# Transposing blocks 7 to 36 of q and k by transfers on SyncE's queue, in a fused sliding-window attention and MLP-mixer kernel

## Chip, cores and metric

One core of one Trainium2 chip runs the whole program. The metric is the device time of one execution in microseconds (us). Three runs of the kernel before took 337.27, 339.30 and 339.14 us; their median is 339.14 us.

## What is computed

Two stages, of which the first feeds the second. Inputs q, k and v have the shape (8, 8, 576, 64): batch, heads, positions, head size.

```python
scores = scale * np.matmul(q, k.transpose(0, 1, 3, 2))
...
bias = slopes[:, None, None] * (-np.abs(rel).astype(np.float32))[None, :, :]
mask = (rel >= 0) & (rel < window)          # window = 128
...
return np.matmul(attn, v).astype(np.float32)
...
xt = x.transpose(0, 2, 1)                   # x: heads side by side, (8, 576, 512)
h = np.maximum(xt @ w_tok1, 0.0) @ w_tok2
u = x + h.transpose(0, 2, 1)
h2 = np.maximum(u @ w_ch1, 0.0) @ w_ch2
return (u + h2).astype(np.float32)
```

Attention looks back over at most 127 positions, so a block of 128 queries needs the keys and values of its own block and of the one before.

## The kernel before

**Blocks.** A sequence of 576 positions is four blocks of 128 and a tail of 64. Two batches make a pair, and their two tails share one block (`TAIL`). So there are nine blocks in a pair and 36 in all. The list `todo` fixes their order (line 97: blocks 0, 1, 2, 3, 7, TAIL, 4, 5, 6 of a pair, then the next pair). This document numbers them 1 to 36 in that order. Blocks 1 to 9 are those of batches 0 and 1, blocks 10 to 18 those of batches 2 and 3, and so on. The key blocks that the attention of batch 0 needs are blocks 1 to 6, that of batch 1 adds 7 to 9.

**Loads.** `load` (lines 80 to 95) brings one block of q, k and v from HBM into `qld`, `kld` and a ring of 14 v tiles. All loads are issued by GpSimd (POOL), which also casts float32 to bfloat16 on the way. A q, k or v load of a full block writes 128 KB. The pool `ld` has 12 buffers for each of `qld` and `kld`, so a block's load waits until the transposes of the block twelve before have read their tile. At most eight of these transfers are under way, since each waits for the landing of the eighth before it.

**Transposes.** Scores need q and k with the head size on the partitions. `transposes` (lines 190 to 202) makes eight TensorE transposes of 128x128 into one PSUM tile `tp` (line 195) and one VectorE copy to the tile `qkT` in SBUF (line 201). The pool `tp` has eight buffers of `qkT`.

**Attention.** `scores` (line 204) multiplies keys by queries into PSUM (line 219), takes exp on ScalarE (line 228) and multiplies by a mask on VectorE (line 231). `values` multiplies by v (line 252) and normalises into the tile `xb` (lines 255, 257).

**Token mix and channel mix.** `token_mix(b)` runs over `xb` (matmuls `t1`, line 303, and `ht`, line 321), adds the residual on VectorE (`ub`, line 322) and transposes it (`ut`, line 327; copy `uT`, line 333). `channel_mix(b)` multiplies by WC1 into `ct` (line 347) or, for a tail, `cx` (line 356), applies Relu on ScalarE (line 349), multiplies by WC2 into `o2` (line 365), adds the residual on VectorE into the tile `ob` (line 369), and stores `ob` from SyncE's queue (SP; lines 372 and 374). The pool `op` has three `ob` tiles: the VectorE addition for a fourth block waits until the first block's store has landed. The PSUM pool `ps_m` has three buffers, shared by `t1`, `ht`, `ct`, `cx` and `o2`.

**Order of the work.** The program interleaves `channel_mix(b)` with attention and token mix of batch b+1 (`interleave`, line 386). A scheduler then sets the final order of every engine's instructions from times that it assumes for them; each engine runs its instructions strictly in that order. A transfer is issued by its engine as an instruction in the same order: SP and POOL stand still until the waits of the instruction at the head are met. In the kernel before, SP issues nothing but the 40 output stores.

Of the kernel before, what the change touches and what calls it, by code (L numbers as in the profile page):

```python
# [11 lines left out]
BF16 = mybir.dt.bfloat16  # L12
# [4 lines left out]
def kernel(  # L17
# [15 lines left out]
    nc = tc.nc  # L33
    P = nc.NUM_PARTITIONS
# [9 lines left out]
    NHP = H // 2  # L44
# [7 lines left out]
    HEADS = [[0, 2, 4, 6], [1, 3, 5, 7]]  # L52

    const = ctx.enter_context(tc.tile_pool(name="const", bufs=1))
    ld = ctx.enter_context(tc.tile_pool(name="ld", bufs=12))
    tpool = ctx.enter_context(tc.tile_pool(name="tp", bufs=8))
    ppool = ctx.enter_context(tc.tile_pool(name="pp", bufs=3))
    small = ctx.enter_context(tc.tile_pool(name="small", bufs=4))
    xpool = ctx.enter_context(tc.tile_pool(name="xp", bufs=2))
# [35 lines left out]
        return got  # L95

    ORDER = [0, 1, 2, 3, 7, TAIL, 4, 5, 6]
    todo = [(pr, blk) for pr in range(B // 2) for blk in ORDER]
    loaded = {}

    def load_to(n):
        while len(loaded) < min(n, len(todo)):
            key = todo[len(loaded)]
            loaded[key] = load(*key)
# [82 lines left out]
    qkT = {}  # L187
    xs = {}

    def transposes(pr, blk):  # L190
        got = loaded[pr, blk]
        tp = ps_o.tile([P, 2 * NHP, P], BF16, name="tp", tag="o")
        for i, t in enumerate(("q", "k")):
            for hp in range(NHP):
                nc.tensor.transpose(  # L195
                    tp[:, i * NHP + hp, :],
                    got[t][:, 2 * hp : 2 * hp + 2, :].rearrange("p h d -> p (h d)"),
                    ident[:, :],
                )
        t = tpool.tile([P, 2 * NHP, P], BF16, name="qkT", tag="qkT")  # L200
        nc.vector.tensor_copy(out=t[:, :, :], in_=tp[:, :, :])  # L201
        qkT[pr, blk] = t

    def scores(pr, blk):

        tail = blk == TAIL
        first = 0 if tail or blk % NC else 1
        me = qkT[pr, blk]
        sp = [ps_s[e].tile([P, 4, 2, P], F32, name=f"sp{e}", tag="s") for e in range(2)]

        work = [(1, blk, 0, P)]
        if tail:
            work += [(0, NC - 1, 0, R), (0, 2 * NC - 1, R, P)]
        elif not first:
            work += [(0, blk - 1, 0, P)]
        for i in range(4):
            for kind, kb, c0, c1 in work:
                for e in range(2):
                    nc.tensor.matmul(  # L219
                        sp[e][:, i, kind, c0:c1],  # L220
                        lhsT=qkT[pr, kb][e * D : (e + 1) * D, NHP + i, :],
                        rhs=me[e * D : (e + 1) * D, i, c0:c1],
                        start=True, stop=True,
                    )
        pb = []
        for e in range(2):
            pe = ppool.tile([P, 4, 2, P], BF16, name=f"pe{e}", tag=f"pe{e}")
            nc.scalar.activation(out=pe[:, :, first:, :], in_=sp[e][:, :, first:, :],  # L228
                                 func=ACT.Exp, scale=scale)
            mk = (maskt if tail else masks)[e]  # L230
            nc.vector.tensor_tensor(out=pe[:, :, first:, :], in0=pe[:, :, first:, :],  # L231
                                    in1=mk[:, :, first:, :], op=ALU.mult)
            pb.append(pe)
        return pb

    def values(pr, blk, e, pe):
        xb = xs[pr]
        tail = blk == TAIL
        vme = loaded[pr, blk]["v"]
        ot = ps_o.tile([P, 4, D + 1], F32, name="ot", tag="o")  # L240
        mms = [(slice(0, P), pe[:, i, 1, :], vme[:, h, :], i) for i, h in enumerate(HEADS[e])]
        if tail:
            for j in range(2):
                vb = loaded[pr, (j + 1) * NC - 1]["v"]
                for i, h in enumerate(HEADS[e]):
                    mms.append((slice(j * R, (j + 1) * R), pe[:, i, 0, j * R : (j + 1) * R],
                                vb[:, h, :], i))
        elif blk % NC:
            vb = loaded[pr, blk - 1]["v"]
            mms += [(slice(0, P), pe[:, i, 0, :], vb[:, h, :], i) for i, h in enumerate(HEADS[e])]  # L250
        for m, (to, l, r, i) in enumerate(mms):
            nc.tensor.matmul(ot[to, i, :], lhsT=l, rhs=r, start=m == 0, stop=m == len(mms) - 1,  # L252
                             skip_group_check=True)
        rt = small.tile([P, 4, 1], F32, name="rt", tag="rt")
        nc.vector.reciprocal(out=rt[:, :, :], in_=ot[:, :, D : D + 1])  # L255
        x4 = xb[:, blk, :].rearrange("p (i e d) -> p i e d", i=4, e=2)
        nc.vector.tensor_tensor(out=x4[:, :, e, :], in0=ot[:, :, 0:D],  # L257
                                in1=rt[:, :, :].broadcast_to([P, 4, D]), op=ALU.mult)
# [3 lines left out]
    def attention(b):  # L262
        pr, half = b // 2, b % 2
        if half == 0:
            xs[pr] = xpool.tile([P, NB, DM], BF16, name="xb", tag="xb")
        units = SCORE_ORDER[half]
        trs = [ORDER[:6], ORDER[6:]][half]
        n = pr * NB + (6 if half else 0)
        wait = list(trs)
        held = None  # L270
        for u in units + [None]:
            need = [] if u is None else ([u, 2 * NC - 1] if u == TAIL else [u])
            while any((pr, w) not in qkT for w in need):
                t = wait.pop(0)
                n += 1
                load_to(n + 7)
                transposes(pr, t)
                yield 450
            got = None
            if u is not None:  # L280
                got = (u, scores(pr, u))
                yield 700
            if held is not None:
                for e in range(2):
                    values(pr, held[0], e, held[1][e])
                    yield 300
            held = got
# [89 lines left out]
    def side(b):  # L377

        yield from attention(b)
        yield from token_mix(b)  # L380
# [21 lines left out]
    load_to(9)  # L402
    load_channel_weights(1)
    drain(attention(0))
    drain(token_mix(0))
    for b in range(B):
# [32 lines left out]
```

## Time and profile before

| | |
|---|---|
| median of three runs | 339.14 us (337.27 to 339.30) |
| the profiled execution's own time | 335.55 us |
| its span, first to last instruction | 333.8 us |
| granted TensorE clock, mean | 0.987 |
| busy: TensorE 303.6, VectorE 169.7, ScalarE 136.9, GpSimd 111.0 us | 91%, 51%, 41%, 33% of the span |
| moved by DMA | 27.81 MB in 121917 packets |

The profile is of one execution. PE is TensorE's matmuls, PEld its weight loads, DVE VectorE, ACT ScalarE, POOL GpSimd and SP SyncE; POOLq and SPq are those engines' instruction queues. In a row that groups instructions, the columns are: line, engine, operation, output<-input, shape and count; then busy time and the mean nanoseconds of one; then the idle time of the engine just before these instructions and what ended it. A row of the timeline has the start, the duration, and in brackets an idle gap before it. A matmul's duration in a row includes its pipeline, so the distance of two starts tells what one costs. In the strips of the page the span is cut into 40 slices of 8.35 us, and each digit is a share in tenths.

The program has three parts: up to 46.5 us the loads, the first attention and the first token mix; then channel mixes with the next batch's attention and token mix beside them, 33.4 and 40.8 us in turn; from 302.7 us the last channel mix alone.

### The profile page before, as it was taken

What the parts mean: (1) busy time and instruction counts of PE and PEld (TensorE: products, weight loads), DVE (VectorE), ACT (ScalarE), POOL (GpSimd) and SP (SyncE); (2) the same over time, 40 slices, a digit from 0 to 9 for tenths busy, and PEclk for the clock granted to TensorE, in tenths of its full rate; (3) what the DMA queues carried; (4) which work ended last, traced back from release to release, by engine and by line L of the source; (5) the groups of instructions that cost most, each with busy time, mean ns of one, the idle gap of its engine ahead of it and who ended that gap; (6) DMA issues with size and microseconds to landing.
All of it is one profiled execution on the core that took longest, in us unless ns stands there. A gap on an engine that the chain in (4) does not pass through costs nothing.

```text
span 333.8 us, 6457 instructions
## 1 busy us (share of the span) xinstructions
PE 303.6 (91%) x2688; PEld 162.6 (49%) x2688; DVE 169.7 (51%) x378; ACT 136.9 (41%) x213; POOL 111.0 (33%) x146
## 2 busy tenths in 40 slices
PE   2457769999999999999999999999999999999993
PEld 1234335545555555455565555455654555455541
DVE  2354456563665636474656546464656447461021
ACT  1653227702774038602863047504772057404600
POOL 8998565888786033303472000000000000000000
PEclk9999599999999999999999999999999999999998
DMA  9999999999999359914999220011000220011022
GB/s 74 136 114 167 170 195 161 139 117 189 174 105 131 75 110 77 67 44 101 73 85 83 81 78 3 0 63 66 2 2 13 83 63 2 0 65 63 2 76 82
DMA packets 121917, 27.81 MB, mean 83 GB/s; under 512 B 113824, under 2 KB 117280, under 8 KB 121888
## 3 DMA queue, kind: packets, MB, share of 16 engines
q0 software_dynamic: 116640, 17.97, 76.1%
q1 hardware_dynamic: 5248, 9.44, 8.2%
q8 instruction: 21, 0.34, 0.4%
q14 instruction: 8, 0.07, 0.1%
HBM read 35.91 MB, written 9.44 MB: 136 GB/s over the span
## 4 chain that ended last, share of the span: by engine, by line
PE 84%; DVE 7%; ACT 4%; issue 1%; DMA 1%; POOL 1%; POOLq 0%
PE o L365 28%; PE ct L347 23%; PE sp L219 7%; PE tp L195 6%; PE ot L252 6%; PE t L303 5%; PE ht L321 5%; PE cx L356 3%; PE ut L327 3%; ACT pe L228 2%; DVE xb L257 2%; DVE pe L231 2%; DVE ub L322 1%; DMA kld<-in_k_dram 1%; DVE qkT L201 1%
## 5 line engine op out<-in xcount | busy, mean ns | idle before, releaser
L349 ACT ACTIVATE r<-ct 128x512 bf16<-128x512 f32 x96 | 56.0, 601 | 133.9 <-PE ct L347 133.9
L347 PE MATMUL ct<-uT,WC 128*128 128x512 bf16 x384 | 98.0, 379 | 0.5 <-DVE uT L333 0.5
L365 PE MATMUL o<-WC,r 128*128 128x512 bf16 x384 | 95.4, 379 | 0.4
L228 ACT ACTIVATE pe<-sp 128x1024 bf16<-128x1024 f32 (+1 forms) x72 | 63.0, 926 | 27.3 <-PE sp L219 27.3
L365 PEld LDWEIGHTS <-r 128*128 128x128 bf16 x384 | 36.0, 98 | 37.6 <-issue 1.9
L91 POOL DMA_DIRECT2D qld<-in_q_dram x40 | 35.6, 891 | 45.3 <-PE tp L195 39.3
L369 DVE TENSOR_TENSOR ob<-o,ub 128x512 f32<-128x512 f32 x36 | 24.8, 690 | 48.1 <-PE o L365 48.1
L347 PEld LDWEIGHTS <-WC 128*128 128x128 bf16 x384 | 33.5, 98 | 28.0 <-issue 0.6
L231 DVE TENSOR_TENSOR pe<-pe,mask 128x1024 bf16<-128x1024 bf16 (+1 forms) x64 | 39.0, 619 | 12.1 <-ACT pe L228 8.0
L201 DVE COPY qkT<-tp 128x1024 bf16<-128x1024 bf16 x36 | 24.9, 692 | 31.5 <-PE tp L195 31.5
L94 POOL DMA_DIRECT2D v<-in_v_dram x40 | 35.0, 881 | 15.1 <-PE ot L252 6.2
L92 POOL DMA_DIRECT2D kld<-in_k_dram x40 | 35.4, 884 | 8.3 <-DMA WC<-in_moe_w_ch_dram 5.8
L322 DVE TENSOR_TENSOR ub<-ht,xb 128x512 bf16<-128x512 f32 x36 | 24.0, 688 | 27.1 <-PE ht L321 26.7
L252 PE MATMUL ot<-v,pe 128*128 128x65 bf16 (+1 forms) x544 | 30.4, 201 | 6.7 <-DVE pe L231 3.5
L252 PEld LDWEIGHTS <-pe 128*128 128x128 bf16 (+1 forms) x544 | 22.4, 102 | 26.6 <-DVE xb L257 17.1
L257 DVE TENSOR_TENSOR xb<-ot,rt 128x256 bf16<-128x256 f32 x72 | 30.6, 425 | 2.5
L219 PE MATMUL sp<-qkT 64*128 64x128 bf16 (+1 forms) x544 | 24.6, 224 | 4.0 <-DVE qkT L201 3.1
L255 DVE RECIPROCAL rt<-ot 128x4 f32<-128x4 f32 x72 | 12.9, 179 | 26.1 <-PE ot L252 25.5
L219 PEld LDWEIGHTS <-qkT 64*128 64x128 bf16 x544 | 17.6, 98 | 17.6 <-DVE qkT L201 16.6
L303 PE MATMUL t<-xb,W 128*128 128x512 bf16 x80 | 23.4, 402 | 0.8 <-DVE xb L257 0.8
L195 PE MATMUL tp<-ident,qld 128*128 128x128 bf16 x144 | 14.8, 228 | 9.1 <-DMA qld<-in_q_dram 5.0
L321 PE MATMUL ht<-r,W 128*128 128x512 bf16 x64 | 19.4, 398 | 0.3 <-ACT r L305 0.3
(46 smaller groups left out, 179.4 us busy)
## 6 DMA issues: line engine op xcount, KB each, us to landing
out_dram<-ob SPq DMA_DIRECT2D x32, 256.0 KB, 2.0
qld<-in_q_dram POOLq DMA_DIRECT2D x32, 128.0 KB, 5.5
kld<-in_k_dram POOLq DMA_DIRECT2D x32, 128.0 KB, 5.6
v<-in_v_dram POOLq DMA_DIRECT2D x32, 128.0 KB, 5.5
WC<-in_moe_w_ch_dram POOLq DMA_DIRECT2D x4, 768.0 KB, 10.4
out_dram<-ob SPq DMA_DIRECT2D x8, 128.0 KB, 2.3
qld<-in_q_dram POOLq DMA_DIRECT2D x8, 64.0 KB, 4.6
kld<-in_k_dram POOLq DMA_DIRECT2D x8, 64.0 KB, 4.2
```

The costliest lines, as they stand in the source:

```text
L91: nc.gpsimd.dma_start(out=got["q"][p0 : p0 + n, :, :], in_=rows(q, b, s0, n))
L92: nc.gpsimd.dma_start(out=got["k"][p0 : p0 + n, :, :], in_=rows(k, b, s0, n))
L219: nc.tensor.matmul(sp[e][:, i, kind, c0:c1], lhsT=qkT[pr, kb][e * D : (e + 1) * D, NHP + i, :], rhs=me[e * D : (e + 1) * D, i, c0:c1], sta ...
L228: nc.scalar.activation(out=pe[:, :, first:, :], in_=sp[e][:, :, first:, :], func=ACT.Exp, scale=scale)
L231: nc.vector.tensor_tensor(out=pe[:, :, first:, :], in0=pe[:, :, first:, :], in1=mk[:, :, first:, :], op=ALU.mult)
L252: nc.tensor.matmul(ot[to, i, :], lhsT=l, rhs=r, start=m == 0, stop=m == len(mms) - 1, skip_group_check=True)
L257: nc.vector.tensor_tensor(out=x4[:, :, e, :], in0=ot[:, :, 0:D], in1=rt[:, :, :].broadcast_to([P, 4, D]), op=ALU.mult)
L303: nc.tensor.matmul(t1[:, :], lhsT=W1[:, c, j * P : (j + 1) * P], rhs=xb[:, blk, :], start=n == 0, stop=n == len(ks) - 1)
L321: nc.tensor.matmul(ht[:, :], lhsT=l, rhs=r, start=n == 0, stop=n == len(mms) - 1)
L347: nc.tensor.matmul(ct[:, :], lhsT=WC1[:, cb, t * P : (t + 1) * P], rhs=uT[:, cb, :], start=cb == 0, stop=cb == NCB - 1)
L349: nc.scalar.activation(out=r2[:, t, :], in_=ct[:, :], func=ACT.Relu)
L365: nc.tensor.matmul(o2[:, :], lhsT=l, rhs=WC2[:, t, :], start=t == 0, stop=t == NHT - 1)
```

## The change

From block 7 on, TensorE's eight transposes and VectorE's copy of a block give way to two transposing transfers, one of q and one of k, each of a 128x512 bfloat16 tile in SBUF to half a `qkT` tile. SP issues them. They stand four blocks ahead of their use in the program's order. Blocks 1 to 6 stay as they were. `ld` has 9 buffers in place of 12, and `tp` 11 in place of 8.

```diff
-    ld = ctx.enter_context(tc.tile_pool(name="ld", bufs=12))
-    tpool = ctx.enter_context(tc.tile_pool(name="tp", bufs=8))
+    ld = ctx.enter_context(tc.tile_pool(name="ld", bufs=9))
+    tpool = ctx.enter_context(tc.tile_pool(name="tp", bufs=11))
...
+    EARLY = 6
...
+    moved = [EARLY]
+
+    def transpose_to(n):
+
+        while moved[0] < min(n, len(todo)):
+            key = todo[moved[0]]
+            moved[0] += 1
+            t = tpool.tile([P, 2 * NHP, P], BF16, name="qkT", tag="qkT")
+            for i, x in enumerate(("q", "k")):
+                nc.sync.dma_start_transpose(
+                    out=t[:, i * NHP : (i + 1) * NHP, :],
+                    in_=loaded[key][x][:, :, :].rearrange("p h d -> p (h d)"),
+                )
+            qkT[key] = t
...
-            while any((pr, w) not in qkT for w in need):
+            while any(w in wait for w in need):
                 t = wait.pop(0)
                 n += 1
                 load_to(n + 7)
-                transposes(pr, t)
-                yield 450
+                transpose_to(n + 4)
+                if (pr, t) not in qkT:
+                    transposes(pr, t)
+                    yield 450
```

The scheduler makes a new order of this. Three places of it matter below. Lines of the changed kernel are 1 to 18 higher than those of the kernel before: L214 is the transposing transfer, L235 the scores, L268 the values, L387 the addition into `ob`, L392 the store. In brackets stand the semaphores that an instruction waits for: DMAHW is the landing of a transfer that SP issued, DMASW of one that POOL issued, and the others are engines.

**SP, where the stores of batch 0 stand.** Before, SP's queue begins with them:

```order
L434 UNCONDITIONAL_BRANCH [waits barrier_Pool_Activation_PE_DVE_SP_release]
L374 DMA out_0_dram<-ob_961 128x512 [waits DVE_49]
L374 DMA out_0_dram<-ob_1011 128x512 [waits DVE_49]
L374 DMA out_0_dram<-ob_1033 128x512 [waits DVE_49]
L374 DMA out_0_dram<-ob_1049 128x512 [waits DVE_49]
```

Now 28 transposing transfers, of blocks 7 to 20, stand ahead of them; these are the last two of blocks 19 and 20 each, the four stores, and the first of block 21:

```order
L214 DMA_TRANSPOSE qkT_1294<-qld_1133 128x4x128 [waits DMAHW0_49,DMASW6_49,PE_49]
L214 DMA_TRANSPOSE qkT_1294<-kld_1134 128x4x128 [waits DMAHW1_49,DMASW7_49]
L214 DMA_TRANSPOSE qkT_1607<-qld_1213 128x4x128 [waits DMAHW2_49,DMASW0_49]
L214 DMA_TRANSPOSE qkT_1607<-kld_1214 128x4x128 [waits DMAHW3_49,DMASW1_49]
L392 DMA out_0_dram<-ob_965 128x512 [waits DMAHW4_49,DVE_49]
L392 DMA out_0_dram<-ob_1005 128x512 [waits DMAHW5_49,DVE_49]
L392 DMA out_0_dram<-ob_1021 128x512 [waits DMAHW6_49,DVE_49]
L392 DMA out_0_dram<-ob_1037 128x512 [waits DMAHW7_49,DVE_49]
L214 DMA_TRANSPOSE qkT_1640<-qld_1281 128x4x128 [waits DMAHW0_49,DMASW3_49,PE_49]
```

The store of `ob_965`, batch 0's first, comes behind the transfer of `kld_1214`, which waits (DMASW1) for the load of block 20's k.

**VectorE, at the end of batch 0's channel mix.** Before, the fourth addition into an `ob` tile is followed by the copies of blocks 10 and 11:

```order
L369 TENSOR_TENSOR ob_1033<-o2_1020,ub_562 128x512 [waits PE_49]
L369 TENSOR_TENSOR ob_1049<-o2_1036,ub_562 128x512 [waits DMAHW0_49,DVE_49,PE_49]
L201 COPY qkT_1075<-tp_1066 128x1024 [waits PE_49]
L201 COPY qkT_1113<-tp_1104 128x1024 [waits PE_49]
L231 TENSOR_TENSOR pe0_1087<-pe0_1087,mask0_141 128x4x128 [waits Activation_49]
```

Now:

```order
L387 TENSOR_TENSOR ob_1021<-o2_1008,ub_574 128x512 [waits PE_49]
L387 TENSOR_TENSOR ob_1037<-o2_1024,ub_574 128x512 [waits DMAHW4_49,DVE_49,PE_49]
L247 TENSOR_TENSOR pe0_1067<-pe0_1067,mask0_141 128x4x128 [waits Activation_49]
L247 TENSOR_TENSOR pe1_1070<-pe1_1070,mask1_142 128x4x128 [waits Activation_49]
L247 TENSOR_TENSOR pe0_1105<-pe0_1105,mask0_141 128x1024 [waits Activation_49]
```

The copies are gone. In both, the fourth addition waits for the landing of batch 0's first store (DMAHW0 before, DMAHW4 now).

**TensorE, at the values of block 4 in batch 0's attention.** Before, the second half of the heads follows the first at once:

```order
L252 MATMUL ot_506<-v2_98,pe0_412 128x65
L252 LDWEIGHTS pe0_412
L252 MATMUL ot_506<-v2_98,pe0_412 128x65
L252 LDWEIGHTS pe1_415 [waits DVE_49]
L252 MATMUL ot_518<-v3_99,pe1_415 128x65 [waits PE_49]
```

Now the scores of block 7 (`qkT_319`) stand between:

```order
L268 MATMUL ot_518<-v2_98,pe0_418 128x65
L235 LDWEIGHTS qkT_319 [waits DMAHW0_49,DMAHW1_49]
L235 MATMUL sp0_646<-qkT_319 128x128 [waits Activation_49]
L235 LDWEIGHTS qkT_319
L235 MATMUL sp0_646<-qkT_319 128x128
L268 LDWEIGHTS pe1_421 [waits DVE_49]
L268 MATMUL ot_530<-v3_99,pe1_421 128x65 [waits PE_49]
```

The scores of blocks 7, 8 and 9 all come ahead of batch 0's `ht` matmuls now; before, they came after the first `ct` matmuls.

## The prediction

> **What bounds the kernel now.** I read the page's busy times first, then the stages, then TensorE's timeline at a transposed block, and last the transfers.
>
> ```profile
> span 333.8 us, 6457 instructions
> PE 303.6 (91%) x2688; PEld 162.6 (49%) x2688; DVE 169.7 (51%) x378; ACT 136.9 (41%) x213; POOL 111.0 (33%) x146
> ```
> ```profile
> 34.00:41.00 7.00, 5.08 (x39) 2.24 (x36) 2.86 (x9) 1.75 (x3) 3.49 (x5) 0.55 2.10 170
> 46.50:80.10 33.60, 33.38 (x275) 17.14 (x275) 18.31 (x40) 14.46 (x22) 24.62 (x30) 1.00 2.07 153
> 80.10:120.90 40.80, 40.35 (x399) 22.23 (x398) 23.16 (x49) 17.98 (x27) 22.06 (x27) 1.00 1.52 128
> ```
>
> The second fence is the table by stage: stretch, its length, busy time of PE, PEld, DVE, ACT and POOL, the granted clock, the DMA share. From 46.5 us on, TensorE is busy for 99% of each stretch and VectorE for little more than half. So TensorE bounds the kernel there, and what leaves TensorE shortens it, if what replaces it is never late. Two blocks in TensorE's timeline:
>
> ```profile
> 33.78 0.42 PE L252 MATMUL ot<-v,pe 128*128 128x65 bf16 x8 [0.74 <-DVE xb L257]
> ...
> 39.46 2.91 PE L321 MATMUL ht<-r,W 128*128 128x512 bf16 x8 [0.26 <-ACT r L305]
> ...
> 46.51 1.02 PE L347 MATMUL ct<-uT,WC 128*128 128x512 bf16 x4 [0.52 <-DVE uT L333]
> ```
> ```profile
> 47.37 0.39 PE L195 MATMUL tp<-ident,qld 128*128 128x128 bf16 x4
> 47.59 0.39 PE L195 MATMUL tp<-ident,kld 128*128 128x128 bf16 x4
> 47.81 1.03 PE L347 MATMUL ct<-uT,WC 128*128 128x512 bf16 x4
> 48.77 0.40 PE L219 MATMUL sp<-qkT 64*128 64x128 bf16 x8
> 49.10 0.40 PE L195 MATMUL tp<-ident,qld 128*128 128x128 bf16 x4
> ```
>
> From the first of a block's eight transposes (47.37) to the next other matmul (47.81) is 0.44 us.
>
> **What the change removes.** Thirty blocks by 0.44 us is 13.2 us of TensorE. VectorE loses 30 copies:
>
> ```profile
> L201 DVE COPY qkT<-tp 128x1024 bf16<-128x1024 bf16 x36 | 24.9, 692 | 31.5 <-PE tp L195 31.5
> ```
>
> That is 20.8 us, which I count as nothing: VectorE is idle for almost half of each stage, and TensorE's matmuls already lie over it. Without that cover it would be worth up to those 20.8 us more.
>
> **What it adds: 60 transfers.** The trace has no transposing transfer, so I bound the cost on the DMA engines of one of 128 KB.
>
> ```profile
> q0 software_dynamic: 116640, 17.97, 76.1%
> q1 hardware_dynamic: 5248, 9.44, 8.2%
> ```
> ```profile
> GB/s 155 151 153 155 158 155 152 156 151 157 158 152 154 155 152 158 155 154 152 155 155 158 153 151 157 154 156 158 253 144 147 144 147 146 142 142 147 155 154 154
> ```
>
> The stores take 8.2% of 16 engines over 333.8 us, 27.4 us for 9.44 MB (36 times 256 KB): 0.76 us each, 0.38 us for 128 KB. The second fence is the transfer rate from 55 to 61 us, loads alone: 131,072 bytes at 155 GB/s is 0.85 us, in 1024 pieces of 128 bytes. If a transpose's time hides in gaps, its price is nothing. It moves 512 pieces of 256 bytes, half the load's pieces, hence 0.42 us, near the store's. I take 0.42, and keep 0 and 0.85 for the range. Advanced Engine Details and Errata (the Trainium skill, X-Bar Transpose) says that transposing transfers on this chip are as fast as plain ones, 350 to 400 GB/s; by it one would be 0.33 to 0.37 us, and the sum below about 2 us less; no run here shows it yet.
>
> **What it moves: SP's queue.** Before, SP only waited for results. Now batch 0's first store stands behind block 20's transposes, and those wait for block 20's loads. When do they land?
>
> ```profile
> 78.56 0.88 POOL L91 DMA_DIRECT2D qld<-in_q_dram  x1
> 79.69 0.89 POOL L92 DMA_DIRECT2D kld<-in_k_dram  x1 [0.24 <-issue]
> ```
> ```profile
> qld<-in_q_dram POOLq DMA_DIRECT2D x1, 128.0 KB, 8.4
> kld<-in_k_dram POOLq DMA_DIRECT2D x1, 128.0 KB, 8.3
> ```
> ```profile
> 70.67 48.71 SPq L374 DMA_DIRECT2D out_dram<-ob  x8
> 121.64 1.17 SPq L372 DMA_DIRECT2D out_dram<-ob  x2
> ```
>
> Block 20's k is issued at 79.69 and lands 8.3 us later, at 88.0; batch 0's first store was issued at 70.67. So the store waits for a load that lands 17 us after the store was wanted. POOL works with few gaps, so the loads cannot come much earlier. In the changed kernel: 88.0, less one v load that now follows (0.85), less the four stores that no longer precede (4 x 0.76 = 3.0), plus the 26 transposes of blocks 7 to 19 on the same engines (26 x 0.42 = 10.9): 95.0. Then the issue of the last transpose and of the store, 0.6 us (two issues in 1.17 us), and the store's flight:
>
> ```profile
> out_dram<-ob SPq DMA_DIRECT2D x4, 256.0 KB, 5.9
> ```
> ```profile
> out_dram<-ob SPq DMA_DIRECT2D x8, 256.0 KB, 2.0
> ```
>
> The first row is 70 to 81 us, with loads under way; the second 144 to 195 us, mostly without. Loads of blocks 21 to 25 are still going, so 5.9: the store lands at 101.5. Behind it stands VectorE: the fourth `ob` addition needs that landing (three buffers), and every mask and normalisation of the next attention is queued behind that addition. On TensorE the third `ct` group needs the PSUM buffer that the addition frees.
>
> ```profile
> 80.13 0.69 DVE L369 TENSOR_TENSOR ob<-o,ub 128x512 f32<-128x512 f32 x1 [1.90 <-PE o L365]
> ```
> ```profile
> 79.93 1.03 PE L347 MATMUL ct<-uT,WC 128*128 128x512 bf16 x4
> 80.79 0.39 PE L195 MATMUL tp<-ident,qld 128*128 128x128 bf16 x4
> ...
> 82.52 0.40 PE L195 MATMUL tp<-ident,qld 128*128 128x128 bf16 x4
> 82.76 0.39 PE L195 MATMUL tp<-ident,kld 128*128 128x128 bf16 x4
> 82.98 0.38 PE L347 MATMUL ct<-uT,WC 128*128 128x512 bf16 x1
> ```
>
> The third group began at 82.98. Now it begins at 101.5 + 0.7 = 102.2, 19.2 us late. After a stop TensorE runs slower: in 34 to 41 us above, with gaps, the granted clock was 0.55. I add 2 us for a restart (about 4 us at half speed, an estimate from that row; 0 to 3.5 in the range).
>
> **An earlier stop, inside the same delay.** TensorE reaches block 7's scores at about 33.8 us, before its loads have landed:
>
> ```profile
> 27.55 1.30 POOL L92 DMA_DIRECT2D kld<-in_k_dram  x1
> ...
> 37.49 0.87 POOL L92 DMA_DIRECT2D kld<-in_k_dram  x1 [2.86 <-DMA WC<-in_moe_w_ch_dram]
> ```
> ```profile
> kld<-in_k_dram POOLq DMA_DIRECT2D x2, 128.0 KB, 11.8
> ```
> ```profile
> kld<-in_k_dram POOLq DMA_DIRECT2D x1, 128.0 KB, 7.1
> ```
>
> Block 7's k lands at 27.55 + 11.8 = 39.4, block 9's at 37.49 + 7.1 = 44.6. With 4 us for a transpose's flight (between the store's 2.0 and 5.9), TensorE goes on at 43.4, 9.6 us late; block 9's transpose lands at 48.6, while the chain from 33.78 to 39.46 brings TensorE there at 49.1. Four masks of 0.69 us then stand in VectorE's chain to the first `ct`: 12.4 us late in all. Work that now lies before it is saved later: three blocks' transposes (1.3) and their scores with block 5's (0.33 for 8 matmuls, so about 2.0 for 56). With blocks 10 and 11 (0.9) the third `ct` group could start at 82.98 + 12.4 - 4.2 = 91.2. The store lands later than that, so this stop costs nothing of its own; without the blocked store it is what is left.
>
> **Later stores.** Batch 1's stand behind block 25's transposes, but were wanted only at
>
> ```profile
> 109.12 10.26 SPq L374 DMA_DIRECT2D out_dram<-ob  x4
> ```
>
> and come 20 us later now, while the first burst of loads ended by 117 us, the fourteenth slice of 8.35 us of the page's DMA strip:
>
> ```profile
> DMA  9999999999999359914999220011000220011022
> ```
>
> With the transposes it ends by about 128. From there on SP is ahead, and I cost later waits at nothing; each that came late would stop VectorE in the same way. The smaller `ld` pool makes POOL wait for SP's transposes, but of blocks some nine earlier, 24 us of loads at 0.88 us, so nothing; without that cover the loads would come later, as in the range's upper part.
>
> **The sum.** At the third `ct` group +19.2 + 2 = +21.2 us; from there 25 blocks (12 to 36) are saved, 25 x 0.44 = -11.0. Net +10.2. Against the profiled execution's own 335.55 us (1.75 outside its span) that is 345.8. The runs' median is 339.14, 3.6 above the profiled one, so I predict 339.14 + 10.2 = 349 us.
>
> **Rivals.**
> *No blocked store, only the early stop.* If transposes cost the DMA engines next to nothing and the store lands in 2 us, the third group starts at 91.2, plus 1 for the clock: +9.2 - 11.0 = -1.8, 337 us. For it: hidden loads leave gaps. Against it: with 0 for a transpose the store still waits for 84.2 (88.0 - 0.85 - 3.0), then 0.6 and 2 to 5.9.
> *The gain in full.* Both stops vanish and 13.2 us go: 326 us, faster. It needs block 20's k landed by 77 us, 7 to 18 sooner than the 84 to 95 above, and block 7's 8 to 10 sooner. Against it: POOL's issues, nearly back to back at 0.88 us. For it: TensorE's full stages.
> *The engines of the transfers become the bound.* If a transpose writes 32-byte strips, 4096 of them at the load's price a piece (0.85 / 1024), it takes 3.4 us. Block 20's k then lands at 84.1 + 26 x 3.4 = 172.5, the third group starts at 180: +97 + 2 - 11 = +88, 427 us. It decides above about 0.9 us each. Nothing in the trace speaks for strips; nothing excludes them. VectorE: DVE Perf Modes (the Trainium skill, The three transpose paths) gives 1309 ns for a 128x128 square by transfer against 390 ns on TensorE, and its rules for authors prefer TensorE where PSUM may be the target, as here. By that figure, if the four squares of a transfer ran one after the other, a transfer would be 5.2 us, an estimate beyond this rival's 3.4; no run here shows it yet.
>
> **How the numbers follow.** Blocked store: 0.68. Early stop only: 0.14. Full gain: 0.07. Transfers as the bound: 0.11. The blocked store's own range: at 0.2 us each and a 3 us store the third group starts at 93.6 (84.1 + 5.2 + 0.6 + 3 + 0.7), with 1 for the clock +0.6, 340; at 0.85 us it starts at 113.5, +21.5, 361. The early stop reaches down to 337, so 337 to 362 leaves out the full gain and dear transfers. About 1% (3.4 us) is what a measurement here can tell from no change. Faster by more: 0.07 and a fifth of the early stop, 0.10. Within it: the rest of the early stop and the low tenth of the blocked store, 0.18. Slower: 0.72.
>
> **What would show it.** Right: SP's first store of batch 0 issued 10 us or more after its `ob` is ready, VectorE waiting at L387 on a transfer for over 5 us near 90 to 102 us, TensorE idle there and at 34 to 43 us, and later pairs about 4 us shorter than 74.2 (33.4 + 40.8). Wrong: store 1 issued before 88 us; a transposing transfer that holds SP or the engines for over 1 us; later stages that do not shrink, which would mean that TensorE was not their bound.

## The result, and the profile after

The changed kernel takes 362.16 us (median of four runs, 360.00 to 363.28) against 338.31 us for the kernel before on the same chip: 1.0698 times as long, 95% interval 1.0633 to 1.0762. That is +23.9 us where +10.2 was forecast. The direction and the two stops are as forecast; most sizes are not. Its profiled execution took 362.28 us.

The page of the changed kernel, span, busy times and transfer queues:

```profile
span 360.5 us, 6047 instructions
PE 297.3 (82%) x2404; PEld 159.4 (44%) x2448; DVE 150.8 (42%) x348; ACT 137.7 (38%) x213; POOL 110.7 (31%) x146
...
q0 software_dynamic: 116640, 17.97, 76.9%
q1 hardware_dynamic: 37888, 17.31, 25.7%
```

TensorE has less work and a smaller share: 82% in place of 91%. The queue q1, which held stores alone, now carries 32,640 more packets, 544 for each of the 60 transfers.

The same execution by stage; each stretch runs from the first `ct` of one channel mix to that of the next (stretch, length, PE, PEld, DVE, ACT, POOL, granted clock, DMA share, GB/s):

```profile
0.00:71.01 71.01, 30.00 (x294) 18.80 (x299) 23.63 (x68) 21.18 (x35) 49.05 (x73) 1.00 1.76 139
71.01:99.84 28.83, 28.62 (x191) 13.78 (x195) 13.44 (x31) 9.87 (x16) 19.17 (x23) 1.00 2.04 150
99.84:153.79 53.95, 41.64 (x346) 23.12 (x350) 19.20 (x43) 18.34 (x27) 31.42 (x38) 0.84 2.11 162
153.79:186.27 32.48, 31.87 (x246) 16.28 (x250) 17.30 (x38) 14.51 (x22) 7.01 (x8) 1.00 1.05 119
186.27:225.21 38.94, 37.73 (x345) 20.87 (x350) 19.23 (x43) 17.91 (x27) 4.04 (x5) 1.00 0.54 82
```

The same table for two later stretches of the kernel before:

```profile
120.72:154.14 33.42, 33.20 (x275) 17.04 (x274) 19.00 (x41) 14.46 (x22) 8.77 (x10) 1.00 0.73 72
154.14:194.94 40.80, 40.35 (x400) 22.25 (x399) 23.16 (x49) 17.98 (x27) 15.47 (x19) 1.00 0.90 85
```

Before, the front took 46.51 us, and then came 33.42 and 40.79 us in turn. So the loss lies in two places: the front (+24.5 us) and the stretch from 99.84 us (+13.2). The stretch between them is 4.6 us shorter, since scores that stood in it now lie in the front and three blocks' transposes are gone. Each later stretch is shorter, by 0.95 us with three blocks in it and by 1.85 us with six: 0.31 us per block.

**First stop.** TensorE's timeline in the front:

```profile
39.93 0.62 PE L268 MATMUL ot<-v,pe 128*128 128x65 bf16 x8
50.12 0.39 PE L235 MATMUL sp<-qkT 64*128 64x128 bf16 x2 [9.57 <-DMA qkT<-kld]
...
57.12 0.71 PE L235 MATMUL sp<-qkT 64*128 64x128 bf16 x10 [3.57 <-DMA qkT<-kld]
...
61.83 1.03 PE L235 MATMUL sp<-qkT 64*128 64x128 bf16 x8 [1.50 <-DMA qkT<-kld]
...
71.01 2.32 PE L365 MATMUL ct<-uT,WC 128*128 128x512 bf16 x10 [0.55 <-DVE uT L351]
```

Three waits, each for the transpose of a `kld` tile: blocks 7, 8 and 9. The six transposes were issued at 39.7 to 47.8 us and landed 8.1, 9.1, 11.1, 12.2, 14.3 and 13.9 us later.

The granted clock of 1.00 that the table gives for the front does not fit TensorE's rows there:

```profile
37.16 0.59 PE L196 MATMUL tp<-ident,qld 128*128 128x128 bf16 x4
...
66.04 0.39 PE L345 MATMUL ut<-ident,ub 128*128 128x128 bf16 x4
```

Four transposes of 128x128 took 0.59 us at 37.16 and 0.39 from 66.04 on, and six `ht` matmuls from 62.79 us on started 0.42 us apart, where such matmuls later start 0.22 us apart. So TensorE seems to have run near half speed in much of the front, to about 65 us; what that cost is not measured.

**Second stop.** The chain of waits over the same execution, at block 20's transposes and batch 0's first store:

```profile
91.28 12.94 DMA qld<-in_q_dram
104.24 1.19 SPq L214
105.52 1.29 SPq L214
106.90 6.45 DMA out_dram<-ob
```

Block 20's load flies 12.9 us, SP issues the two transposes, 1.3 us apart, and only then the store. VectorE's timeline shows the first and the fourth addition:

```profile
91.29 0.69 DVE L387 TENSOR_TENSOR ob<-o,ub 128x512 f32<-128x512 f32 x1 [0.22 <-PE o L383]
...
113.47 0.69 DVE L387 TENSOR_TENSOR ob<-o,ub 128x512 f32<-128x512 f32 x1 [15.33 <-DMA out_dram<-ob]
```

and TensorE's timeline the third `ct` group behind it:

```profile
114.21 0.59 PE L365 MATMUL ct<-uT,WC 128*128 128x512 bf16 x1 [11.08 <-DVE ob L387]
```

The first `ob` was ready at 91.98; its store went out 14.9 us later. The table by stretch, TensorE alone, gives what followed the stop (the column before the DMA share is the granted clock):

```profile
106.10:114.20 8.10, 0.00 (x0) 0.50 1.72 202
114.20:123.20 9.00, 8.76 (x67) 0.50 2.02 175
123.20:130.00 6.80, 6.10 (x94) 1.00 2.22 149
```

After the stop TensorE ran 9.0 us at half clock, some 4.5 us lost (an estimate: half of 9.0).

### The profile page after: what moved, and what is told of

Its sections match the earlier page's. It is cut to its first block, busy times and chain, and to the rows that moved or that the text cites. A ratio compares the mean times of both kernels' runs of the same rounds, so it can differ in the third digit from the quotient of the medians.

```text
span 360.5 us, 6047 instructions
## 1 busy us (share of the span) xinstructions
PE 297.3 (82%) x2404; PEld 159.4 (44%) x2448; DVE 150.8 (42%) x348; ACT 137.7 (38%) x213; POOL 110.7 (31%) x146
## 4 chain that ended last, share of the span: by engine, by line
PE 54%; DMA 16%; POOL 9%; ACT 7%; issue 6%; DVE 5%; SPq 2%; ACTq 0%; POOLq 0%; DVEq 0%
PE o L383 23%; PE ct L365 13%; DMA qld<-in_q_dram 11%; ACT pe L244 6%; PE ht L339 4%; DMA qkT<-kld 4%; PE t L321 4%; PE ot L268 3%; DVE pe L247 3%; PE cx L374 3%; PE sp L235 3%; POOL v L94 2%; SPq L214 2%; POOL kld L92 2%; POOL qld L91 2%
## 5 line engine op out<-in xcount | busy, mean ns | idle before, releaser
L367 ACT ACTIVATE r<-ct 128x512 bf16<-128x512 f32 x96 | 57.0, 605 | 143.8 <-PE ct L365 139.0
L365 PE MATMUL ct<-uT,WC 128*128 128x512 bf16 x364 | 96.8, 384 | 13.1 <-DVE ob L387 11.1
L383 PE MATMUL o<-WC,r 128*128 128x512 bf16 x372 | 89.4, 379 | 0.6
L387 DVE TENSOR_TENSOR ob<-o,ub 128x512 f32<-128x512 f32 x36 | 24.9, 691 | 74.8 <-PE o L383 59.5
L235 PE MATMUL sp<-qkT 64*128 64x128 bf16 (+1 forms) x544 | 34.1, 235 | 18.4 <-DMA qkT<-kld 14.6
L235 PEld LDWEIGHTS <-qkT 64*128 64x128 bf16 x544 | 22.8, 104 | 35.7 <-DMA qkT<-kld 16.6
L268 PE MATMUL ot<-v,pe 128*128 128x65 bf16 (+1 forms) x544 | 31.4, 204 | 7.6 <-DVE xb L273 3.9
L268 PEld LDWEIGHTS <-pe 128*128 128x128 bf16 (+1 forms) x544 | 23.7, 105 | 24.1 <-DVE xb L273 14.5
L321 PE MATMUL t<-xb,W 128*128 128x512 bf16 x73 | 22.2, 402 | 7.4 <-DMA W<-in_moe_w_tok_dram 6.0
L351 DVE COPY uT<-ut 128x512 bf16<-128x512 bf16 x32 | 13.5, 422 | 8.4 <-PE ut L345 8.4
L345 PEld LDWEIGHTS <-ub 128*128 128x128 bf16 x144 | 10.9, 97 | 9.5 <-issue 0.8
```

Source lines behind the costliest of these rows:

```text
L235: nc.tensor.matmul(sp[e][:, i, kind, c0:c1], lhsT=qkT[pr, kb][e * D : (e + 1) * D, NHP + i, :], rhs=me[e * D : (e + 1) * D, i, c0:c1], sta ...
L321: nc.tensor.matmul(t1[:, :], lhsT=W1[:, c, j * P : (j + 1) * P], rhs=xb[:, blk, :], start=n == 0, stop=n == len(ks) - 1)
L365: nc.tensor.matmul(ct[:, :], lhsT=WC1[:, cb, t * P : (t + 1) * P], rhs=uT[:, cb, :], start=cb == 0, stop=cb == NCB - 1)
L367: nc.scalar.activation(out=r2[:, t, :], in_=ct[:, :], func=ACT.Relu)
L383: nc.tensor.matmul(o2[:, :], lhsT=l, rhs=WC2[:, t, :], start=t == 0, stop=t == NHT - 1)
```

## The experiments

**Theory.** Two stops make the loss: the scores of blocks 7 to 9 wait for their transposes, and batch 0's stores stand in SP's queue behind block 20's. Elsewhere the change gains 0.31 us per block. **Rivals:** the traffic of the 60 transfers is the cause, wherever it stands; the smaller `ld` pool is; the steady part loses. The kernel before, run beside each group of experiments, took 337.7 to 338.6 us.

**One stop at a time.**

```diff
-    opool = ctx.enter_context(tc.tile_pool(name="op", bufs=3))
+    opool = ctx.enter_context(tc.tile_pool(name="op", bufs=8))
```

> The changed kernel with eight output tiles `ob` in place of three; nothing else differs. Two-stops theory (TensorE stops once for the late transposes of blocks 7 to 9 and once because batch 0's stores stand behind block 20's transposes): the second stop goes, since VectorE's fourth addition needs no landed store. First `ct` stays at 71 us (the changed kernel: 71.0), the second phase falls from 53.95 to about 39 us like the later ones (38.9), and the time from 362 to about 347 us. SP issues batch 0's stores as late as before (about 107 us). Rival 1, the transfers' traffic itself (the transposes slow the loads, and the loads set the pace): the time stays above 355. Rival 3, TensorE pays in the steady part for something other than a store: the second phase stays above 48 us.

Measured: 349.83 us, some 3 us more than expected. First `ct` at 70.97, second phase 38.88 us, the first store still issued only at 104.92. The second stop is gone, and 12.3 us with it.

```diff
-    EARLY = 6
+    EARLY = 9
```

> The changed kernel with blocks 1 to 9 left on TensorE and VectorE (EARLY 9 in place of 6); three `ob` tiles as in the change. Two-stops theory: the front goes back to the kernel before (first `ct` at 46.5 to 48 us in place of 71.0), but the stores of batch 0, wanted near 70 us, still stand behind block 20's transposes, which come near 98 to 104 us; so the second stop grows to about 25 us, and the time falls only to about 354 us (350 to 359). If the two stops were independent, it would fall by the whole 24.5 us of the front, to 338. Rival 1 (traffic): first `ct` stays late, above 55 us.

Measured: 353.09 us. First `ct` at 49.80. VectorE's fourth addition in this kernel:

```profile
105.84 0.69 DVE L387 TENSOR_TENSOR ob<-o,ub 128x512 f32<-128x512 f32 x1 [24.31 <-DMA out_dram<-ob]
```

The front came back by 21.2 us, and the time fell by only 9.1: the second stop took up the rest, from 15.3 to 24.3 us of VectorE waiting. The two stops overlap; the later landing decides. It came sooner here: block 20's k landed at 97.48 us, where it was 104.95 in the change.

> The changed kernel with both edits: blocks 1 to 9 on TensorE, and eight `ob` tiles. Two-stops theory: no stop is left, only the saving of 27 blocks by about 0.31 us = 8.4 us; about 330 us, below the kernel before (338). First `ct` at 46.5 to 48 us, phases of about 32.5 and 38.9 us in turn. Rival 1 (traffic): the same 54 transfers move beside the same loads, scores wait for late transposes, 340 or more. Rival 3 (the steady part gains nothing): 338.

Measured, with both edits: 331.53 us, 0.9801 of the kernel before (0.9776 to 0.9826). Had the two stops been independent, the two gains would have added up to 12.3 + 9.1 = 21.4 us and left 340.8. Later stretches of 32.49 and 38.95 us are as expected; the first `ct`, at 49.05, is 1 us later than expected.

> The changed kernel with 12 buffers of `qld` and `kld` again, as in the kernel before. Rival 2 (the smaller pool holds the loads back until SP's transposes have read the tiles, and so makes everything late): loads of blocks 10 to 20 land earlier, and the time falls to 350 us or less. Two-stops theory: POOL waits less, but the transposes of blocks 7 to 9 fly as long and the stores stay behind block 20's transposes; 358 to 363 us, the same within 1%.

Measured: 360.50 us with `bufs=12` for `ld`; first `ct` at 70.41, the first store issued at 104.87. The pool is not the cause; the 1.7 us that it may be worth is within the spread of the runs.

**Is it the traffic?** Two kernels on the side of the kernel before. The control changes only `op` to eight buffers there:

> The kernel before with eight `ob` tiles in place of three, nothing transposed by transfers: the control for the kernels with eight tiles. In the kernel before the stores go out as soon as their `ob` is ready and VectorE waits on no transfer for long, so two-stops theory: the same as before, 337 to 340 us. If the tiles alone help, as a rival for the 331.5 us of the kernel with both edits would need: about 332.

Measured: 338.32 us, ratio 1.0003 (0.9970 to 1.0037). So the 331.5 us are not the tiles' doing.

The other keeps all of TensorE's transposes and VectorE's copies, and makes the 60 transfers as well, into tiles that nothing reads (the lines are shown against `transpose_to` of the change):

```diff
+    dpool = ctx.enter_context(tc.tile_pool(name="dp", bufs=3))
...
-            t = tpool.tile([P, 2 * NHP, P], BF16, name="qkT", tag="qkT")
+            t = dpool.tile([P, 2 * NHP, P], BF16, name="dup", tag="dup")
...
-            qkT[key] = t
```

> The kernel before's TensorE transposes and VectorE copies for all 36 blocks, and beside them the 60 transposing transfers of the change, into tiles that nothing reads (three of them); 9 `qld`/`kld` buffers, eight `ob` tiles. It does work twice, so its time is read against the kernel before, as the price of the traffic alone. Two-stops theory: the transfers cost DMA engine time that is mostly spare, nobody waits for their landing: 338 to 343 us. The last load lands later by 60 times what one transposing transfer costs the engines: 25 us at 0.42, 60 us at 1.0. Rival 1 (the traffic is the cause): 350 us or more.

Measured: 338.40 us, ratio 0.9992 (0.9954 to 1.0031), and later stretches of 33.42 and 40.79 us as in the kernel before. The same traffic, waited for by nobody, costs nothing. It does delay the loads: block 20's k landed at 113.1 us (86.9 in the control), the last load at 213.5 (185.1). The last load comes 28.4 us later, 0.47 us for each of 60 transfers, which taken alone would speak for the smaller price. But it is no measure of the price: the later loads have slack, since GpSimd waits 39.6 us in the control, and 41.2 us here, for TensorE's transposes to free `qld` tiles.

**Another issuer for the stores.** `nc.sync.dma_start` becomes `nc.scalar.dma_start` at both stores of `channel_mix`.

> The changed kernel with the output stores issued from ScalarE's queue in place of SyncE's; three `ob` tiles as in the change. Two-stops theory: what holds the stores back is their place behind the transposes in SP's order, so the second stop goes here as it did with eight tiles: second phase about 39 to 41 us (53.95 in the change), first `ct` at 71, the time about 348 us (346 to 352). If three tiles are too few in themselves (a store's flight of 6 to 7 us is too long beside the transfers), the second phase stays above 45 us and the time above 354.

Measured: 355.47 us, 7 above what was expected; second phase 42.19. Of the two signs that three tiles are too few in themselves, the time above 354 us came and the phase above 45 us did not. ScalarE's timeline in this kernel:

```profile
90.17 0.60 ACT L367 ACTIVATE r<-ct 128x512 bf16<-128x512 f32 x1 [0.70 <-PE ct L365]
98.62 9.44 ACTq L392 DMA_DIRECT2D out_dram<-ob  x4
108.10 0.60 ACT L367 ACTIVATE r<-ct 128x512 bf16<-128x512 f32 x1 [17.34 <-DMA out_dram<-ob]
```

The first store goes out 8.3 us sooner than in the change (98.62 against 106.90), and VectorE waits 5.0 us in place of 15.3. But ScalarE now stands 17.3 us at its stores, with Relus of `ct` queued behind. Against the kernel with eight tiles its profiled span is 7.8 us longer (5.6 by the medians): 1.5 in the front, 1.3 and 3.3 in the next two stretches, 1.7 later. The head of the line moved to another engine; it was not removed: the fourth addition still waits for the first store, which landed 8.25 us after its issue.

**How many tiles?** With blocks 1 to 9 on TensorE, `op` gets four buffers.

> Blocks 1 to 9 on TensorE as in the kernel with both edits, and four `ob` tiles in place of eight (three gave 353.1 us, eight 331.5). Two-stops theory: only the fourth addition ever needs the late store; with four tiles the next one that needs a landed store is batch 1's first, some 29 us into its phase (about 114 us), and batch 0's first store lands at 109. So one tile is worth the whole stop: 331 to 333 us. If the tiles help by degrees, because flights of 6 to 8 us are long for few tiles, four are near three: 345 to 350.

Measured: 342.70 us. My expectation missed a stop. VectorE's waits, and SP's timeline, in this kernel:

```profile
DVE ob L387 <- DMA out_dram<-ob: 12.8, 2, 10.9
```
```profile
123.95 1.19 SPq L214 DMA_TRANSPOSE qkT<-qld  x1
125.23 1.23 SPq L214 DMA_TRANSPOSE qkT<-kld  x1
126.56 2.42 SPq L392 DMA_DIRECT2D out_dram<-ob  x4
```

The fifth addition waits for nothing, as expected. The ninth, batch 1's fifth, needs batch 1's first store, and that stands behind block 25's transposes: it was issued at 126.56 though its `ob` was written by 114.3. It lands at 133.06, and the third phase is 43.13 us in place of 32.48. The prediction had named this queue and costed it at nothing; with three tiles and later phases it did cost nothing.

> Blocks 1 to 9 on TensorE, five `ob` tiles (three gave 353.1 us, four 342.7, eight 331.5). With four, the ninth addition (batch 1's fifth) stood 10.9 us for batch 1's first store, which SP issued at 126.6 behind block 25's transposes. With five, the addition that needs that store is batch 2's first, some 20 us later, and none is late: third phase back from 43.1 to 32.5 us, 331 to 333 us. If tiles help by degrees: 336 to 339.

Measured: 330.39 us, 0.9763 (0.9727 to 0.9800), third phase 32.48. The fifth tile removes it whole, and VectorE waits for no store in this kernel, so tiles do not help by degrees: the fourth and the fifth each cover one late store.

> The same with 12 buffers of `qld` and `kld`. If the smaller load pool costs something once the stops are gone: 2 us or more faster than with 9. Two-stops theory: the same within 1%, 330 to 333 us.

Measured: 330.62 us. The load pool costs nothing here either.

**Where is the rest of the saving?** In place of the two transfers, `transpose_to` sets `qkT[key] = qkT[0, key[1]]`.

> The kernel with both edits, with its 54 transposing transfers left out: the scores of blocks 10 to 36 read the transposed tiles of blocks 1 to 9, so its output is not the reference's. It shows what the transfers cost where nobody should wait for them. Two-stops theory: TensorE gains nothing more, since it waits for no transfer now: later phases stay at 32.5 and 38.9 us in turn, 329 to 332 us in all; the missing 0.13 us per block (0.31 saved, 0.44 removed) lies in TensorE's own order. If late or dear transfers are what keeps the saving at 0.31: phases of 32.1 and 38.1 us and about 328 us or less.

Measured: 329.60 us. The table by stretch in this kernel, and behind it that of the kernel with both edits, for the same two stretches:

```profile
122.16:154.64 32.48, 31.87 (x247) 16.27 (x251) 17.28 (x38) 14.52 (x22) 4.61 (x6) 1.00 0.65 77
154.64:193.56 38.92, 37.73 (x346) 20.88 (x350) 19.22 (x43) 17.91 (x27) 4.01 (x5) 1.00 0.31 48
```
```profile
123.64:156.13 32.49, 32.39 (x251) 16.25 (x250) 17.29 (x38) 14.51 (x22) 16.16 (x20) 1.00 1.88 175
156.13:195.08 38.95, 38.59 (x352) 20.89 (x350) 19.23 (x43) 17.91 (x27) 12.95 (x16) 1.00 1.69 141
```

The lengths agree to 0.03 us (the busy times differ with the matmul records, in brackets, that are missing). So the transfers are hidden altogether in these stretches, and the missing 0.13 us per block is not theirs. The whole run is 1.9 us shorter without them; in the profiled executions 1.2 us of it lie in the phase after the first `ct` (34.49 in place of 35.71 us), where the recorded half clock ended at 51.0 us and not at 53.9. TensorE's rows in the kernel with both edits point to its order:

```profile
160.55 0.60 PE L235 MATMUL sp<-qkT 64*128 64x128 bf16 x8
...
161.62 0.51 PE L235 MATMUL sp<-qkT 64*128 64x128 bf16 x6
162.06 0.30 PE L268 MATMUL ot<-v,pe 128*128 128x65 bf16 x4
162.29 0.28 PE L235 MATMUL sp<-qkT 64*128 64x128 bf16 x2
```

One block's 16 score matmuls stand in three pieces with other matmuls between, 1.39 us busy; in the kernel before such a block was one piece:

```profile
158.16 0.62 PE L219 MATMUL sp<-qkT 64*128 64x128 bf16 x16
```

In this stage the 80 score matmuls stand in eight pieces in place of five. The kernel without the transfers has the same eight pieces. That the pieces cost the 0.13 us is argued from these rows; no run changed the order alone.

**Why do the front's transposes fly so long?** First, WC2's loads are moved behind the first attention's, with eight `ob` tiles:

```diff
-    load_channel_weights(1)
     drain(attention(0))
+    load_channel_weights(1)
```

> The changed kernel with eight `ob` tiles, and the two loads of WC2 issued after those of blocks 10 to 13 in place of before them. Two-stops theory with the flight as the front's cause (transposes of blocks 7 to 9 flew 8, 9, 11, 12, 14, 14 us while the two large WC2 loads were under way): the later flights fall to 7 to 8 us as those beside block loads do, block 9's k lands near 53 in place of 60 to 62, first `ct` at 62 to 64 us in place of 71, and the time about 342 us (340 to 344; 349.8 with eight tiles alone). If the transposes are slow in themselves in the front, or it is the hoisted scores alone, first `ct` stays at 70 or later and the time at 349.

Measured: 340.47 us, first `ct` at 64.67. Then blocks 7 to 9 are loaded ahead of WC1 as well (`load_to(9)` before `load_channel_weights(0)`), and the same order of loads goes into the kernel before as a control:

> The change (blocks 7 to 36 by transfers) with eight `ob` tiles and another order of loads in the front: blocks 7 to 9 ahead of WC1, and WC2 behind blocks 10 to 13. With WC2 moved alone: 340.5 us, first `ct` at 64.7, of which 8.5 us was the wait for block 7's transposes. Two-stops theory: block 7's loads land about 8 us sooner, its transposes near 41 us in place of 49.1, TensorE waits 1 to 2 us there; first `ct` at 57 to 58, 331 to 335 us, below the kernel before. If the front is late for TensorE's own new order (hoisted scores and first token-mix matmuls), first `ct` stays at 62 or later and the time at 338.

> Control: the kernel before with eight `ob` tiles and that same order of loads. Two-stops theory: nothing in it waits for blocks 7 to 9 in the front, so no gain: 337 to 341 us (WC1, needed at the first `ct` near 46.5, may land a little late). If the order of loads is a gain by itself: 334 or less.

Measured: 340.36 us where 331 to 335 was expected, not below the kernel before, first `ct` at 61.80; the control 338.14. At block 7 TensorE no longer waits for a transpose, as expected, but those of blocks 8 and 9 fall beside WC1's load and fly up to 12.1 us, and from 39.8 to 56.9 us TensorE ran at half clock. I had moved the weight load from one set of transposes to another. The first `ct` came 2.9 us sooner than with WC2 moved alone, and the time stayed the same: TensorE was at half clock again from 60.3 to 67.1 us, and the phase from the first `ct` took 31.35 us in place of 28.82. No run with these blocks on transfers puts their scores back behind the first `ct` matmuls, so how much of the late front is TensorE's new order is open. Last, WC2 stays where it was, in shorter pieces:

```diff
-                nc.gpsimd.dma_start(out=WC2[:, js, :], in_=w[:, js, :])
+                for y in range(4):
+                    cs = slice(y * P, (y + 1) * P)
+                    nc.gpsimd.dma_start(out=WC2[:, js, cs], in_=w[:, js, cs])
```

> The change with eight `ob` tiles (349.8 us), and each of WC2's two loads cut into four by columns: the same bytes at the same place in the order, in runs a quarter as long (128 columns in place of 512). Theory A, the transfer engines serve two queues by turns of pieces, and WC2's long pieces make each turn of a transposing transfer long: the transposes of blocks 7 to 9 land 1.5 to 2.2 us apart as they do beside block loads (2.3 to 3.7 in the change), block 9's k at 54 to 56 in place of 60.5, first `ct` nine to ten us after that, at 64 to 65, the time about 343 us. Theory B, the amount of bytes ahead is what counts: flights of 8 to 15 us stay, first `ct` at 70 or later, the time 349 or more.

Measured: 343.55 us, block 9's k at 54.7 and first `ct` at 66.50, theory A's numbers but for a first `ct` 1.5 us later. The transfer view from 38 to 60 us, of this kernel and then of the one with eight tiles alone (KB each, median us to landing):

```profile
WC<-in_moe_w_ch_dram POOLq DMA_DIRECT2D x8, 192.0 KB, 13.2
...
qkT<-qld SPq DMA_TRANSPOSE x3, 9.0
qkT<-kld SPq DMA_TRANSPOSE x3, 9.2
```
```profile
WC<-in_moe_w_ch_dram POOLq DMA_DIRECT2D x2, 768.0 KB, 16.0
...
qkT<-qld SPq DMA_TRANSPOSE x3, 11.2
qkT<-kld SPq DMA_TRANSPOSE x3, 13.5
```

The same bytes in pieces a quarter as long, and the transposes fly 9 us; WC2 itself was complete at 59.8 us against 58.9. So the number of bytes does not set the flight. The pieces' length is the likely cause, but cutting also made eight transfers of two, issued from 39.7 to 49.0 us in place of 39.8 to 40.7, and no run parts the one from the other. DMA: Bandwidth & Descriptors (the Trainium skill, Queues, rings and completion order) says that an engine takes turns between queues by whole packets. The run fits that, flights of up to 9.4 us in place of 15.3, though no row shows the turns themselves. The front in all kernels with blocks 7 to 36 on transfers:

| kernel | beside the transposes of blocks 7 to 9 | their flights, us | block 9's k landed | first `ct` |
|---|---|---|---|---|
| the change | WC2 | 8.1 to 14.3 | 61.8 | 71.0 |
| eight `ob` tiles | WC2 | 7.1 to 15.3 | 60.5 | 71.0 |
| 12 `ld` buffers | WC2 | 6.8 to 14.1 | 60.1 | 70.4 |
| stores by ScalarE | WC2 | 7.7 to 14.8 | 62.5 | 72.5 |
| WC2 in short pieces | WC2, short | 6.9 to 9.4 | 54.7 | 66.5 |
| WC2 later | block loads | 7.7 to 9.0 | 55.6 | 64.7 |
| blocks 7 to 9 first | WC1 | 7.2 to 12.1 | 51.5 | 61.8 |

The first `ct` comes 9 to 12 us after block 9's k in each.

## Why the prediction was wrong, point by point

**What bounds the kernel, and the two stops: right.** Each stop is where it was put, and taking its cause away removed it. The signs came: batch 0's first store 14.9 us after its `ob`, VectorE 15.3 us in wait up to 113 us, TensorE idle there and up to 50 us.

**The price of a transposing transfer: the step that failed.** "Hence 0.42 us, near the store's. I take 0.42" should have been about the upper end, 0.85. Block 20's k landed at 104.95, not 95.0: by the prediction's own terms (104.95 - 84.15) / 26 = 0.80 us each. A second pair is near: between the kernel with both edits and the same without transfers, that load lands at 99.93 and 85.37, with 18 transposes ahead, (99.93 - 85.37) / 18 = 0.81. Neither is exact. Without transfers the four stores still precede that load, and at the prediction's 3.0 us for them the second figure becomes 0.98; in the change with 12 `ld` buffers the load landed at 101.51, which makes the first 0.67. So 0.7 to 1.0 us is what these runs show, as estimates, and 0.42 lies outside. The table by stage agrees: from 71.01 to 99.84 us, with loads and transposes together, the engines moved 150 GB/s, no more than the 155 of loads alone, where transfers at 0.42 us would have raised the rate. Half the pieces did not make half the time. At 0.85 the prediction put the third `ct` group at 113.5 and the net at +21.5; it came at 114.21.

131,072 bytes in 0.81 us is 162 GB/s. Advanced Engine Details and Errata (the Trainium skill, X-Bar Transpose) has transposing transfers as fast as plain ones, at 350 to 400 GB/s. Beside block loads these runs bear out the first half against the loads (0.85 us), not against the stores (0.38), and do not reach the rate.

**The third `ct` group:** 82.98 became 114.21, +31.2 where +19.2 was forecast. The 12.0 us between them: the load 10.0, SP's issue 1.35 (1.95 us from the load's landing to the store's issue, 0.6 forecast), the store's flight 0.55 (6.45, 5.9 forecast), the addition 0.16. Each transpose holds SP for over 1 us, which the prediction named as a sign against it; here is SP's timeline with few loads under way:

```profile
157.17 1.22 SPq L214 DMA_TRANSPOSE qkT<-qld  x1
158.49 1.22 SPq L214 DMA_TRANSPOSE qkT<-kld  x1
```

**The restart:** 2 us forecast (0 to 3.5), about 4.5 measured.

**The saving:** from the third group on, the span is 246.3 us against 250.8, -4.5 us. With 4.5 lost to the clock that is 9.0 saved for 25 blocks, where 11.0 was forecast. At 0.31 us per block it would be 7.8; 16 score matmuls of block 11, about 0.55 us, moved ahead of the third group, and the rest is not traced. In the undisturbed stretches it is 0.31 us per block and not 0.44, so the pairs are 2.8 us shorter, not 4. The sum: +31.2 - 4.5 = +26.7 in the span. The medians differ by 23.9, since the profiled execution of the kernel before was 2.8 us faster than its median.

**The early stop:** TensorE went on at 50.1 and not 43.4, since the flight was taken as 4 us and was 8 to 14; the first `ct` was 24.5 us late, not 12.4, and without the blocked store (eight tiles) the third group comes at 104.09, not 91.2. "Costs nothing of its own" holds for TensorE's wait in the change, where the store's 114.2 is later than 104.09. It does not hold for the transfers of blocks 7 to 9: with these blocks back on TensorE block 20's k landed 7.5 us sooner (six transposes fewer make 4.9 of it, at 0.81 each) and the time fell by 9.1 us. And "early stop only, 337" was 349.8 on the chip.

**The rivals.** Dear transfers, 3.4 us each: no, by the price above; and with little else moving a whole transfer landed 2.4 us after its issue. VectorE: DVE Perf Modes (the Trainium skill, The three transpose paths) would make it 5.2 us, an estimate from its figure for one square, if the four squares ran one after the other. The 2.4 us say that they do not. The full gain takes blocks 1 to 9 off the transfers and five output tiles: 330.4 us, 7.3 below the kernel before by the medians, where 27 blocks at 0.31 make 8.4. The larger `ld` pool was worth nothing that the runs can tell, as forecast. For VectorE's copies, counted as nothing, no run stands alone; that the saving was 0.31 us per block and not above TensorE's 0.44 gives no sign that they were worth more.

## What to carry to other kernels

A transfer's place in an in-order queue can cost more than the transfer: look for what stands behind it that was ready earlier, and count the buffers that stretch over the gap. Two stops in a row overlap, so removing the first may only lengthen the second; test each alone and both together. When a cost has two bounds and the answer changes within them, a single point is a guess: at the upper bound the same working gave +21.5 us, and the forecast should have leaned that way.

## What the runs showed of the hardware

- A transposing transfer of a 128x512 bfloat16 tile is 544 packets and keeps SP for 1.2 us or more. It lands 2.4 us after its issue when little else moves, 7 to 10 us beside block loads, and up to 15 beside weight loads.
- The flight is shorter beside a queue of shorter pieces: cutting WC2 into runs a quarter as long, in eight transfers in place of two, brought the last transposes from 15 to 9 us, and WC2 came 0.8 us later.
- A stop of 11 to 20 us of TensorE was followed by 9 us at half clock, in the change (114.2 to 123.2 us) and with blocks 7 to 9 back on TensorE (106.6 to 115.6). In the front the recorded clock can mislead: with WC2 later it reads 1.00 after the 8.5 us wait, but eight `ot` matmuls took 0.62 us at 49.49 us and 0.42 at 69.31.
